# One load for the projection's matrix, and the last matrix in pieces of 9, 4 and 1 blocks, in a decoding transformer layer

## The chip, the core and the metric

The kernel runs on one core of a Trainium2 chip. The core has five engines, each with its own stream of instructions: TensorE (PE: matmuls into PSUM, with weight loads, PEld, that overlap them), VectorE (DVE), ScalarE (ACT), GpSimd (POOL) and SyncE (SP, which here only issues DMAs). They are tied together by semaphores. The metric is the device time in microseconds (us); lower is better.

## What is computed

One token passes through one layer of attention over a long cache, and then through a block of normalisation, mixing and MLP. `_layernorm` subtracts the mean and divides by the standard deviation; `_gelu` is the tanh form. All inputs are bfloat16.

```python
# x [1,1,512], k_cache and v_cache [1,8,16384,128], wq [512,4096], wo [4096,512]
q = (x @ wq).reshape(B, Sq, 32, 128).transpose(0, 2, 1, 3)      # x normalised
k, v = repeat(k_cache, 4, axis=1), repeat(v_cache, 4, axis=1)
p = softmax(einsum("bhqd,bhkd->bhqk", q, k) * 128 ** -0.5)
o = einsum("bhqk,bhkd->bhqd", p, v)
A = o.transpose(0, 2, 1, 3).reshape(B, Sq, 4096) @ wo
h = x + A
# B of the normalised h, with w1, w2 [512,512], w3 [512,1792], w4 [1792,512]
...
x1 = x + hs
h2 = _gelu(_layernorm(x1) @ w3) @ w4
out = h + (x1 + h2)
```

With one token the shifted parts of the mixing (`hs`) are all padding, so `hs` is zero, and neither w1 nor w2 is read. What has to be read is the cache (67 MB), wq and wo (4 MB each), and w3 and w4 (1.75 MB each).

## The kernel before

**Loads.** All large loads are issued by SP and go through one data queue, in order: wq, the keys and values of four pairs of heads in turn, then wo, w3 and w4. `load` (line 487) gives every load its name, its destination and its key; a load name has a semaphore of its own, which rises by 16 when the load has landed. wo goes where the keys' first half was (`kb[0]`), w3 and w4 where the second half was (`kb[1]`), so they are issued when VectorE has transposed the last pair's keys out of those buffers. The constants `WO`, `W3`, `W4` (lines 375 to 378) cut the matrices into loads, in units of rows for each partition: wo into 28 and 4 of 32 rows (of 512 columns), w3 into one load, w4 into pieces of 7, 5 and 2 of 14 blocks (of 512 columns, 1 KB for each partition). `piece` tells which load a row or block is in.

**The loops.** For each of four pairs TensorE multiplies transposed keys with the queries (line 666), VectorE and ScalarE make the softmax, TensorE multiplies with the values (line 703), and the result is gathered (lines 714 to 751). TensorE's stream of this part is one loop with registers (`_tensor`, line 176).

**The end.** Behind the loop TensorE first runs *unread* matmuls, whose result nobody reads (line 527): `P.spin(6)` (line 792) makes a loop of 6 passes with two of them in each. Then come:

- the projection: 32 matmuls of `o_b` with wo (line 795), in four column groups of the array, which add up into four 32-partition groups of one PSUM bank; a copy to `osum` (799), and 4 matmuls with `row32` (801) that fold the four groups into the row's layout, 128 partitions by 128 columns;
- the residual and the sums of the row (`row_sums`, 538), more unread matmuls (two of line 527, and a wide one in fp32 of 512 columns, line 535), the centred row `hc` (809);
- 16 matmuls with w3 (815), the variance (`variance`, 556), `xsum` = h + x1 (820), again a wide unread matmul (384 columns), two GELU activations (825), each followed by a transpose on VectorE (829) that makes one half of `hcol`, the columns for w4: blocks 0 to 6 from the first half, 7 to 13 from the second;
- one matmul that starts the output row in `n_ps` with `xsum` (833);
- w4's first 7 blocks: 7 matmuls of 512 columns into `O_ps[1]` in four column groups (838), a copy to `osum` (841), and 4 matmuls that fold it into `n_ps` (846);
- w4's other 7 blocks: for each of them four matmuls of 128 columns, straight into `n_ps` (852);
- two copies of halves of the result, on ACT (857) and DVE (859), the output write (860), and VectorE's wait for it (862).

An fp32 matmul shows as two in the profile (two passes).

**The branch near the end.** `pe(None, ...)` (line 844) and `dve(None)` (832) mark places at which the engine's stream has a compare-and-branch that is never taken back to the loop (`pe_pair`, line 360); its wait (`late`, an activation on ACT, line 842) comes in front of it.

**Semaphores of the engines.** `emit` (line 114) gives each engine one semaphore, that rises with each instruction that somebody waits for; an operation with `own=` counts on another one of that engine. [...]

Of the kernel before, what the change touches and what calls it, by code (L numbers as in the profile page):

```python
# [10 lines left out]
ACTF = mybir.ActivationFunctionType  # L11
# [13 lines left out]
class Program:  # L25
# [88 lines left out]
    def emit(self):  # L114
        for ops in self.ops.values():
            for o in ops:
                for d in o.deps:
                    d.needed = True
        told = {self.place(o) for e in ("PE", "DVE") for o in self.ops[e] if o.needed and o.at}
        for e in ("PE", "DVE"):  # L120
            for o in self.ops[e]:
                o.needed = o.needed or (o.at is not None and self.place(o) in told)
        for e, ops in self.ops.items():
            sems, n = {}, {}
            for o in ops:
                if o.dma is None and o.needed:
                    if o.own not in sems:
                        name = f"e_{e}" if o.own is None else f"e_{e}_{o.own}"
                        sems[o.own] = self.ctx.enter_context(self.nc.semaphore(name))
                    n[o.own] = n.get(o.own, 0) + o.worth  # L130
                    o.sem, o.val = sems[o.own], n[o.own]
        self.nc.switch_bb("body", parent=None)
        for e, eng in (("SP", self.nc.sync), ("ACT", self.nc.scalar), ("POOL", self.nc.gpsimd)):
            self._run(eng, self.ops[e], {})
        self._vector()
        self._tensor()
# [235 lines left out]
NCH = D // 128  # L372
FQ = FM // 4
NHC = FM // 128
WO = ((0, 28), (28, 32))
VP = 1
W3 = ((0, 4),)
W4 = ((0, 7), (7, 12), (12, 14))
NEAR = 7
BLOCK = (0, 2, 1, 3)  # L380
PAIRS = HKV // 2
RPARTS = 9
# [8 lines left out]
def bass_sequential_preLN__gqa_block_cached__mixer_s_mlp__decode_kernel(  # L391
# [13 lines left out]
    with ExitStack() as ctx:  # L405
        sb = lambda name, shape, dt: ctx.enter_context(nc.sbuf_tensor(name, shape, dt))
        ps = lambda name, shape, dt: ctx.enter_context(nc.psum_tensor(name, shape, dt))
        P = Program(nc, ctx)
# [19 lines left out]
        row32 = sb("row32", [128, 32], FP32)  # L428
# [21 lines left out]
        osum = sb("osum", [128, D], FP32)  # L450
# [13 lines left out]
        def late(words, dt=BF16):  # L464
            nonlocal taken
            lo, taken = taken, taken + words * (2 if dt is FP32 else 1)
            part = kt[:, lo:taken]
            return part.bitcast(FP32) if dt is FP32 else part

        o_f, hr, xsum = late(32, FP32), late(128, FP32), late(128, FP32)  # L470
        o_b, hg = late(32), late(FQ)
        hc = late(NCH * 32).rearrange("p (k u) -> p k u", u=32)
        hcol = late(NHC * 32).rearrange("p (m u) -> p m u", u=32)
        fin = late(256)[0:64, :]
        wq_sb, wo_sb = vb, kb[0]
        w3_sb = kb[1][:, 0:NCH * FM].rearrange("p (k f) -> p k f", k=NCH)
        w4_sb = kb[1][:, NCH * FM:2 * NCH * FM].rearrange("p (m c) -> p m c", m=NHC)
# [4 lines left out]
        O_ps = [banks[:, 2, :], banks[:, 3, :]]  # L482
        A_ps, mn_ps = banks[:, 4, :], banks[:, 5, :]
        m_ps, n_ps = mn_ps[:, 0:256], mn_ps[:, 256:512]


        def load(name, dst, src, key, by="SP", also=()):
            P.op(by, lambda e: e.dma_start(dst, src), w=[key, *also], dma=name)  # L488
# [18 lines left out]
        def dve(fn, r=(), w=(), bank=()):  # L507
            return P.op("DVE", fn, r, w, bank)

        def act(fn, r=(), w=(), bank=()):  # L510
            return P.op("ACT", fn, r, w, bank)
# [4 lines left out]
        def pe(fn, r=(), w=(), bank=(), also=()):  # L516

            return P.op("PE", fn, r, w, bank, also=also)

        def piece(cuts, m):  # L520
            return [lo <= m < hi for lo, hi in cuts].index(True)

        def copies(col, n):

            return col.to_broadcast([col.shape[0], n])

        P.unread = lambda e: e.matmul(banks[:, 7, :], copies(xn[:, 0:1], 128), copies(xn[:, 0:1], 512),  # L527
                                      start=True, stop=True)
# [45 lines left out]
        for n, (lo, hi) in enumerate(((0, 2048), (2048, NCH * HQ * DH))):  # L574
# [13 lines left out]
            r=["ident", "x4"], w=["quarter"])  # L588
        pe(lambda e: e.matmul(O_ps[0][:, 0:128], quarter[:, :, :].rearrange("p q u -> p (q u)"), x4[:, :],
                              start=True, stop=True), r=["quarter"], w=[("O", 0)], bank=[("O", 0)])  # L590
# [8 lines left out]
             r=["ident_f"], w=["swapped"])  # L599

        dve(lambda e: e.tensor_reduce(row32[:, :], ident_f[:, :].rearrange("p (c r) -> p r c", c=4), AX.X, ALU.add),
            r=["ident_f"], w=["row32"])
        dve(lambda e: e.tensor_reduce(maskdd[:, :], ident_f[:, :].rearrange("p (n d) -> p d n", d=4), AX.X, ALU.add),
            r=["ident_f"], w=["maskdd"])
# [6 lines left out]
        for z, m, key, mk in ((zo, rowgh, "zo", "rowgh"), (zd, maskgh, "zd", "maskgh")):  # L611
# [5 lines left out]
            r=["hT", (("st", 0), 0), (("st", 0), 6)] + [("v", 0), ("v", 1)], w=["xn"])  # L617
# [3 lines left out]
        for i, key in enumerate(keys):  # L621
            P.part("query", i)
            for k in range(NCH):
                pe(lambda e, k=k: e.matmul(row[:, bass.ds(P.b, 512)], copies(xn[:, k:k + 1], 128),  # L624
                                           wq_k[:, k, bass.ds(P.c, REP * DH)], start=(k == 0), stop=(k == NCH - 1)),
                   r=["xn"], also=[("v", 0), ("v", 1)], w=["n" if key == "mn" else key], bank=[key])
        P.part()
        for g in range(2):
            half = banks[64 * g:64 * g + 64, PAIRS * g:PAIRS * g + PAIRS, :].rearrange("p j c -> p (j c)")
            for b in range(2):  # L630
# [3 lines left out]
                    r=["n" if x == "mn" else x for x in keys[PAIRS * g:PAIRS * g + PAIRS]], w=["qcol"],  # L634
                    bank=keys[PAIRS * g:PAIRS * g + PAIRS])
# [35 lines left out]
        both = dict(bank=[("s", 0), ("s", 1)])  # L671
# [104 lines left out]
        act(lambda e: e.activation(scr[0:1, 1:2], mean4[0:1, 0:1], ACTF.Gelu_apprx_tanh), r=["mean4"], w=["scr"])  # L776
        for n, (lo, hi) in enumerate(WO):
            load(f"wo{n}", wo_sb[:, lo * D:hi * D], A_wo.rearrange("(p r) c -> p (r c)", p=128)[:, lo * D:hi * D],
# [4 lines left out]
        w4_in = B_w4.rearrange("(p m) c -> p m c", p=128)  # L783
        for n, (lo, hi) in enumerate(W4):
            load(f"w4{n}", w4_sb[:, lo:hi, :], w4_in[:, lo:hi, :], ("r", 1, len(W3) + n))
# [3 lines left out]
            r=[("o_m", j) for j in range(PAIRS)], w=["o_f"])  # L789
        dve(lambda e: e.tensor_copy(o_b[:, :], o_f[:, :]), r=["o_f"], w=["o_b"])  # L790

        P.spin(6)
        for r_ in range(32):
            q = r_ % 4
            pe(lambda e, r_=r_, q=q: e.matmul(O_ps[0][32 * q:32 * q + 32, :], copies(o_b[:, r_:r_ + 1], 32),  # L795
                                              wo_sb[:, r_ * D:(r_ + 1) * D], start=(r_ < 4), stop=(r_ >= 28)),
               r=["o_b", ("r", 0, piece(WO, r_))], w=[("O", 0)], bank=[("O", 0)])
        h_ps, hkey = banks[:, 6, :], "spare0"
        dve(lambda e: e.tensor_copy(osum[:, :], O_ps[0][:, :]), r=[("O", 0)], w=["osum"] + [("osum", c) for c in range(4)], bank=[("O", 0)])
        for q in range(4):  # L800
            pe(lambda e, q=q: e.matmul(h_ps[32 * q:32 * q + 32, 0:128], copies(row32[:, 0:1], 32),
                                       osum[:, q * 128:(q + 1) * 128], start=True, stop=True),
               r=["osum", "row32"], w=[hkey], bank=[hkey])
# [6 lines left out]
            r=["hT", (S, 0)], w=["hc"])  # L810


        for k in range(NCH):
            for q in range(4):
                pe(lambda e, k=k, q=q: e.matmul(s_ps[32 * q:32 * q + 32, 0, 0:FQ], hc[:, k, :],  # L815
                                                w3_sb[:, k, q * FQ:(q + 1) * FQ], start=(k == 0), stop=(k == NCH - 1)),
                   r=["hc", ("r", 1, piece(W3, k))], w=[("s", 0)], bank=[("s", 0)])
# [3 lines left out]
            r=["hr", "xs", (S, 6)], w=["xsum"])  # L821
        unread_f(384)
        for n in range(2):
# [9 lines left out]
        pe(lambda e: e.matmul(  # L833
            n_ps[:, 0:128], swapped[:, :], xsum[:, :], start=True, stop=False, skip_group_check=True),
           r=["swapped", "xsum"], w=["n"], bank=["mn"])
        for m in range(NEAR):
            q = m % 4
            pe(lambda e, m=m, q=q: e.matmul(O_ps[1][32 * q:32 * q + 32, :], hcol[:, m, :], w4_sb[:, m, :],
                                            start=(m < 4), stop=(m >= NEAR - 4)),
               r=[("hcol", 2 * m // NHC), ("r", 1, len(W3) + piece(W4, m))], w=[("O", 1)], bank=[("O", 1)])  # L840
        dve(lambda e: e.tensor_copy(osum[:, :], O_ps[1][:, :]), r=[("O", 1)], w=["osum"], bank=[("O", 1)])
        act(lambda e: e.activation(hg[:, 0:256], hcol[:, 0:8, :].rearrange("p m u -> p (m u)"), ACTF.Identity),
            r=[("hcol", 1)], w=["late", ("hg", 0), ("hg", 1)])
        pe(None, r=["late"])
        for o in range(4):
            pe(lambda e, o=o: e.matmul(
                n_ps[32 * o:32 * o + 32, 0:128], copies(row32[:, 0:1], 32),
                osum[:, BLOCK[o] * 128:(BLOCK[o] + 1) * 128], start=False, stop=False,
                skip_group_check=True), r=["osum", "row32"], w=["n"], bank=["mn"])
        for m in range(NEAR, NHC):  # L850
            for o in range(4):
                pe(lambda e, m=m, o=o: e.matmul(
                    n_ps[32 * o:32 * o + 32, 0:128], hcol[:, m, :], w4_sb[:, m, BLOCK[o] * 128:(BLOCK[o] + 1) * 128],
                    start=False, stop=(m == NHC - 1),
                    skip_group_check=True),
                   r=["late", ("r", 1, len(W3) + piece(W4, m))], w=["n"], bank=["mn"])
        act(lambda e: e.activation(fin[:, 0:128], n_ps[0:64, 0:128], ACTF.Identity),
            r=["n"], w=[("fin", 0)], bank=["mn"])
        dve(lambda e: e.tensor_copy(fin[:, 128:256], n_ps[64:128, 0:128]), r=["n"], w=[("fin", 1)])
        P.op("SP", lambda e: e.dma_start(out[0, 0:1, :].rearrange("o (q j) -> (o q) j", q=2), fin[31:33, :]),  # L860
             r=[("fin", 1), ("fin", 0)], w=["out"], dma="out")
        P.op("DVE", lambda e: e.nop(), r=["out"])
# [31 lines left out]
```

## Time and profile before

| | |
|---|---|
| median of three runs | 189.71 us (189.6 to 189.81) |
| the profiled execution: device time | 189.68 us |
| the profiled execution: span of the instructions | 188.2 us |
| TensorE busy | 127.9 us (68%) |
| VectorE busy | 107.9 us (57%) |
| ScalarE, GpSimd busy | 14.2 us (8%), 9.4 us (5%) |
| read from HBM | 79.17 MB, 421 GB/s over the span |

The profile is of one execution. Its times count from the start of the span. In the rows, `out<-in` names the tiles written and read; many late tiles live in the buffer `kt`, and w3 and w4 in `kb`, so they appear under those names. The rows of a timeline have the start, the duration, the engine, the line and the operation, and in brackets how long the engine was idle before and what ended it. SPq is SP's queue of instructions, PEldq TensorE's. The page's list of DMA issues has the size in KB and the median time from issue to landing.

### The profile page before, as it was taken

Reading aid. Unit: us, or ns where it says so; the run is one execution under the profiler, and the core shown is the slowest. Engines: PE = TensorE matmul, PEld = TensorE weight load, DVE = VectorE, ACT = ScalarE, POOL = GpSimd, SP = SyncE. Lnnn points to the kernel's source line nnn. Section 1 sums busy time; section 2 is a strip of 40 time slices with the busy share of each in tenths; the row PEclk is TensorE's granted clock in tenths of the full one; section 3 lists DMA queues with packets and bytes.
Section 4 is the critical chain, followed back from the end, with each engine's and each line's share of the span. In section 5 each row is a group of like instructions: output and inputs, shape, how many; then the busy total and the mean of one; then the engine's idle time right before and its main releaser. Section 6 shows DMA issues by size and latency. Waiting matters only on the chain.

```text
span 188.2 us, 2422 instructions
## 1 busy us (share of the span) xinstructions
PE 127.9 (68%) x776; PEld 53.2 (28%) x780; DVE 107.9 (57%) x138; ACT 14.2 (8%) x32; POOL 9.4 (5%) x21
## 2 busy tenths in 40 slices
PE   1019800699965703999775019997986999797984
PEld 1003300243422201344332003442432334343332
DVE  4300651999645009998450069994659894453254
ACT  3000000000020200000012000000220000320012
POOL 1700000000000020000002100000003000000010
PEclk9999995599997885599999855999998899999999
DMA  6999999999999999888999999997999998799994
GB/s 240 457 418 446 446 446 446 446 446 446 446 446 446 446 446 446 362 376 376 446 446 446 446 446 446 446 446 334 446 446 446 557 446 348 334 471 421 404 410 179
DMA packets 2461, 79.19 MB, mean 421 GB/s; under 512 B 282, under 2 KB 284, under 8 KB 924
## 3 DMA queue, kind: packets, MB, share of 16 engines
q1 hardware_dynamic: 2452, 79.17, 97.9%
q8 instruction: 1, 0.02, 0.0%
q10 hardware_dynamic: 8, 0.00, 0.0%
HBM read 79.17 MB, written 0.00 MB: 421 GB/s over the span
## 4 chain that ended last, share of the span: by engine, by line
DMA 44%; PE 31%; DVE 14%; issue 8%; POOL 1%; SPq 0%; ACT 0%; POOLq 0%; DVEq 0%; ACTq 0%
DMA kb<-in_A_k_cache_dram 30%; PE banks L666 18%; DMA vb<-in_A_v_cache_dram 15%; DVE kt L647 8%; PE banks L527 4%; PE banks L703 4%; DVE pt L692 1%; DVE mx L676 1%; PE banks L795 1%; PE banks L660 1%; DVE od L733 1%; PE banks L680 1%; PE banks L535 1%; PE banks L815 1%; SPq L488 0%
## 5 line engine op out<-in xcount | busy, mean ns | idle before, releaser
L647 DVE STREAM_TRANSPOSE kt<-kb 128x1024 int32<-128x1024 int32 (+1 forms) x49 | 71.8, 1534 | 31.9 <-DMA kb<-in_A_k_cache_dram 31.9
L666 PE MATMUL banks<-kt,qn 128*128 x256 | 67.9, 417 | 0.0
L666 PEld LDWEIGHTS banks<-kt,qn 128*128 x256 | 26.4, 103 | 40.0 <-issue 21.1
L527 PE MATMUL banks<-xn 128*128 128x512 bf16 x90 | 22.0, 381 | 0.6 <-issue 0.6
L660 PE MATMUL banks<-qn 128*128 128x512 bf16 x8 | 3.7, 464 | 26.5 <-DVE kt L647 26.2
L703 PE MATMUL banks<-vb,pt 128*32 128x512 bf16 x256 | 16.3, 411 | 0.0
L624 PE MATMUL banks<-vb,xn 128*128 x32 | 9.2, 459 | 9.6 <-DVE xn L615 9.6
L688 ACT ACTIVATE p_sb<-banks,bias 128x1024 bf16<-128x1024 f32 x4 | 4.5, 1114 | 126.0 <-DVE nmh L684 126.0
L692 DVE STREAM_TRANSPOSE pt<-p_sb 64x1024 bf16<-64x1024 bf16 x8 | 9.9, 1239 | 5.4 <-ACT p_sb L688 5.3
L527 PEld LDWEIGHTS banks<-xn 128*128 128x128 bf16 x94 | 8.8, 99 | 12.1 <-issue 4.5
L676 DVE TENSOR_REDUCE mx<-banks 128x1 f32<-128x1024 f32 x4 | 4.9, 1225 | 9.0 <-PE banks L666 9.0
L703 PEld LDWEIGHTS banks<-vb,pt 128*32 128x32 bf16 x256 | 8.0, 103 | 6.3 <-issue 2.0
L631 DVE STREAM_TRANSPOSE kt<-banks 64x1024 f32<-64x1024 f32 x4 | 4.8, 1227 | 7.2 <-PE banks L624 7.2
L660 PEld LDWEIGHTS banks<-qn 128*128 128x128 bf16 x8 | 0.8, 100 | 28.3 <-issue 28.0
L722 POOL TENSOR_TENSOR osum<-osum 128x256 f32<-128x256 f32 x3 | 2.2, 723 | 127.5 <-ACT osum L719 127.5
L624 PEld LDWEIGHTS banks<-vb,xn 128*128 128x128 bf16 x32 | 3.7, 115 | 14.7 <-issue 12.3
L738 PE MATMUL banks<-od,zo 128*32 128x128 f32 x8 | 1.6, 285 | 7.3 <-POOL od L724 6.1
L680 PE MATMUL banks<-mxd,mean 128*128 128x128 f32 x8 | 2.0, 326 | 5.3 <-DVE mxd L677 5.3
L719 ACT ACTIVATE osum<-banks,rowc 128x128 f32<-128x128 f32 x12 | 3.4, 368 | 20.7 <-PE banks L703 20.7
L615 DVE TENSOR_SCALAR xn<-hT,st 128x4 bf16<-128x4 f32 x1 | 0.3, 290 | 6.5 <-DMA vb<-in_A_wq_dram 6.5
L711 PE MATMUL banks<-acc,zd 128*32 128x1 f32 x8 | 0.9, 180 | 4.1 <-DVE pt L692 4.0
L568 POOL TENSOR_TENSOR st<-st,expo 128x1 f32<-128x1 f32 (+1 forms) x2 | 1.3, 636 | 41.3 <-DVE st L566 41.3
(88 smaller groups left out, 46.3 us busy)
## 6 DMA issues: line engine op xcount, KB each, us to landing
kb<-in_A_k_cache_dram SPq DMA_DIRECT2D x2, 4096.0 KB, 20.4
vb<-in_A_wq_dram SPq DMA_DIRECT2D x1, 3584.0 KB, 11.7
kb<-in_A_wo_dram SPq DMA_DIRECT2D x1, 3584.0 KB, 28.5
kb<-in_B_w_dram SPq DMA_DIRECT2D x1, 1792.0 KB, 24.2
kb<-in_B_w_dram SPq DMA_DIRECT2D x1, 896.0 KB, 26.0
kb<-in_B_w_dram SPq DMA_DIRECT2D x1, 640.0 KB, 27.1
vb<-in_A_wq_dram SPq DMA_DIRECT2D x1, 512.0 KB, 3.6
kb<-in_A_wo_dram SPq DMA_DIRECT2D x1, 512.0 KB, 29.4
```

The lines of the kernel that those rows point to most:

```text
L527: P.unread = lambda e: e.matmul(banks[:, 7, :], copies(xn[:, 0:1], 128), copies(xn[:, 0:1], 512), start=True, stop=True)
L624: pe(lambda e, k=k: e.matmul(row[:, bass.ds(P.b, 512)], copies(xn[:, k:k + 1], 128), wq_k[:, k, bass.ds(P.c, REP * DH)], start=(k == 0), s ...
L631: dve(lambda e, g=g, b=b, half=half: e.transpose(qcol[64 * g:64 * g + 64, 2 * b:2 * b + 2, :, :].rearrange("p e m u -> p (e m u)"), half.r ...
L647: P.op("DVE", lambda e, t=t, n=n, at=at: e.transpose(kt[:, t * KP:(t + n) * KP].bitcast(I32), kb_all[:, at:at + n * KP].bitcast(I32)), r=[ ...
L660: pe(lambda e: e.matmul(row[:, bass.ds(P.y, 512)], copies(none, 128), copies(none, 512), start=True, stop=False, skip_group_check=True), r ...
L666: pe(lambda e, n=n: e.matmul(row[:, bass.ds(P.y, 512)], qn[:, n, bass.ds(P.q, 128)], key_piece(P.k, n), start=False, stop=(n == 3), skip_g ...
L676: dve(lambda e: e.tensor_reduce(mx[:, :], s_all, AX.X, ALU.max), r=[("s", 0), ("s", 1)], w=["mx"], **both)
L680: pe(lambda e: e.matmul(m_ps[:, 0:128], mean4[:, :], mxd[:, :], start=True, stop=True), r=["mxd", "mean4"], w=["m"], bank=["mn"])
L688: act(lambda e: e.activation(p_sb[:, :], s_all, ACTF.Exp, bias=bias[:, 0:1], scale=float(SCALE), accum_out=acc[:, :]), r=[("s", 0), ("s", ...
L692: dve(lambda e, g=g: e.transpose(pt[64 * g:64 * g + 64, :, :, g, :], p_sb[64 * g:64 * g + 64, :]), r=["p"], w=["pt"])
L703: pe(lambda e, l=l, ct=ct, ch=ch: e.matmul(O_ps[0][32 * ct:32 * ct + 32, :], pt[:, l, ch, :, :].rearrange("p g u -> p (g u)"), tiles[:, l ...
L719: act(lambda e, c=c: e.activation(osum[:, c * 128:(c + 1) * 128], O[:, c * 128:(c + 1) * 128], ACTF.Identity, scale=rowc[:, c:c + 1]), r=[ ...
```

## The change

Four things are changed. wo comes in one load. w4 comes in pieces of 9, 4 and 1 blocks. All 14 blocks of w4 are multiplied straight into the row in `n_ps`, four matmuls of 128 columns each, so that the path over `O_ps[1]` and `osum` is gone, with the activation `late`; the branch stands between blocks 8 and 9. The two copies of the result count on one semaphore that both engines share, `both`, so that the output write has one wait. The loop of unread matmuls ahead of the projection has 8 passes.

```diff
@@ emit
+        both, told_both = {}, {}
         for e, ops in self.ops.items():
-            sems, n = {}, {}
+            own_sems, own_n = {}, {}
             for o in ops:
+                sems, n = (both, told_both) if o.own == "both" else (own_sems, own_n)
                 if o.dma is None and o.needed:
...
-WO = ((0, 28), (28, 32))
+WO = ((0, 32),)
 VP = 1
 W3 = ((0, 4),)
-W4 = ((0, 7), (7, 12), (12, 14))
-NEAR = 7
+W4 = ((0, 9), (9, 13), (13, 14))
...
-        P.spin(6)
+        P.spin(8)
...
-        for m in range(NEAR):
-            q = m % 4
-            pe(lambda e, m=m, q=q: e.matmul(O_ps[1][32 * q:32 * q + 32, :], hcol[:, m, :], w4_sb[:, m, :],
-                                            start=(m < 4), stop=(m >= NEAR - 4)),
-               r=[("hcol", 2 * m // NHC), ("r", 1, len(W3) + piece(W4, m))], w=[("O", 1)], bank=[("O", 1)])
-        dve(lambda e: e.tensor_copy(osum[:, :], O_ps[1][:, :]), r=[("O", 1)], w=["osum"], bank=[("O", 1)])
-        act(lambda e: e.activation(hg[:, 0:256], hcol[:, 0:8, :].rearrange("p m u -> p (m u)"), ACTF.Identity),
-            r=[("hcol", 1)], w=["late", ("hg", 0), ("hg", 1)])
-        pe(None, r=["late"])
-        for o in range(4):
-            pe(lambda e, o=o: e.matmul(
-                n_ps[32 * o:32 * o + 32, 0:128], copies(row32[:, 0:1], 32),
-                osum[:, BLOCK[o] * 128:(BLOCK[o] + 1) * 128], start=False, stop=False,
-                skip_group_check=True), r=["osum", "row32"], w=["n"], bank=["mn"])
-        for m in range(NEAR, NHC):
+        for m in range(NHC):
+            if m == W4[0][1]:
+                pe(None, r=[("hcol", 1)])
             for o in range(4):
                 pe(lambda e, m=m, o=o: e.matmul(
                     n_ps[32 * o:32 * o + 32, 0:128], hcol[:, m, :], w4_sb[:, m, BLOCK[o] * 128:(BLOCK[o] + 1) * 128],
                     start=False, stop=(m == NHC - 1),
                     skip_group_check=True),
-                   r=["late", ("r", 1, len(W3) + piece(W4, m))], w=["n"], bank=["mn"])
-        act(lambda e: e.activation(fin[:, 0:128], n_ps[0:64, 0:128], ACTF.Identity),
-            r=["n"], w=[("fin", 0)], bank=["mn"])
-        dve(lambda e: e.tensor_copy(fin[:, 128:256], n_ps[64:128, 0:128]), r=["n"], w=[("fin", 1)])
+                   r=[("hcol", 2 * m // NHC), ("r", 1, len(W3) + piece(W4, m))], w=["n"], bank=["mn"])
+        P.op("ACT", lambda e: e.activation(fin[:, 0:128], n_ps[0:64, 0:128], ACTF.Identity),
+             r=["n"], w=[("fin", 0)], own="both")
+        P.op("DVE", lambda e: e.tensor_copy(fin[:, 128:256], n_ps[64:128, 0:128]), r=["n"], w=[("fin", 1)], own="both")
```

## The prediction

> **What bounds the kernel now.** I read the page first, then the last five microseconds of the timeline, then the issues and landings of the weight loads.
>
> ```profile
> span 188.2 us, 2422 instructions
> q1 hardware_dynamic: 2452, 79.17, 97.9%
> DMA 44%; PE 31%; DVE 14%; issue 8%; POOL 1%; SPq 0%; ACT 0%; POOLq 0%; DVEq 0%; ACTq 0%
> ```
>
> The one data queue is busy for 97.9% of the span. All 79 MB must pass through it, so unless a part of the change opens a hole in it or shortens its sum, the time can move only by what happens after the last byte. The end of the timeline (start, duration, engine, and in brackets what ended the idle time):
>
> ```profile
> 183.49 1.04 DVE L829 STREAM_TRANSPOSE kt<-kt 128x224 bf16<-128x224 bf16 x2 [0.44 <-ACT kt L825]
> 184.16 0.61 PE L838 MATMUL banks<-kb,kt 128*32 128x512 bf16 x7 [0.18 <-DVE kt L829]
> 184.82 0.69 DVE L841 COPY osum<-banks 128x512 f32<-128x512 f32 x1 [0.29 <-PE banks L838]
> 185.56 0.43 PE L846 MATMUL banks<-osum,row 128*32 128x128 f32 x8 [0.79 <-DVE osum L841]
> 185.81 0.78 PE L852 MATMUL banks<-kb,kt 128*32 128x128 bf16 x28
> 186.29 0.12 PEld L852 LDWEIGHTS banks<-kb,kt 128*32 128x32 bf16 x8 [0.19 <-DMA kb<-in_B_w_dram]
> 186.64 0.27 ACT L857 ACTIVATE kt<-banks 64x128 bf16<-64x128 f32 x1 [1.66 <-PE banks L852]
> 186.64 0.29 DVE L859 CAST kt<-banks 64x128 bf16<-64x128 f32 x1 [1.13 <-PE banks L852]
> 186.98 0.33 SPq L860 DMA_DIRECT2D out_dram<-kt  x1
> ```
>
> The sixth row decides: at 186.29 TensorE had finished 20 of its 28 last matmuls and stood still for 0.19 us until the last piece of w4 landed. The chain of compute (transposes, seven wide matmuls, copy, fold, 20 matmuls) is done 0.19 us before the data. From 186.29 on the path is fixed: the last matmuls, two copies side by side, the output write, the end at 188.15. So two terms set the end: when the last piece lands, and what stands behind it.
>
> **The landings.** Issue times on SP's queue, and the microseconds from issue to landing (last column of the page's list of DMA issues):
>
> ```profile
> 147.74 0.33 SPq L488 DMA_DIRECT2D kb<-in_A_wo_dram  x1
> ...
> 148.12 0.43 SPq L488 DMA_DIRECT2D kb<-in_A_wo_dram  x1
> ...
> 157.64 0.33 SPq L488 DMA_DIRECT2D kb<-in_B_w_dram  x1
> ...
> 158.02 0.43 SPq L488 DMA_DIRECT2D kb<-in_B_w_dram  x1
> ...
> 158.49 0.44 SPq L488 DMA_DIRECT2D kb<-in_B_w_dram  x1
> ...
> 158.98 0.44 SPq L488 DMA_DIRECT2D kb<-in_B_w_dram  x1
> ```
> ```profile
> kb<-in_A_wo_dram SPq DMA_DIRECT2D x1, 3584.0 KB, 28.5
> kb<-in_B_w_dram SPq DMA_DIRECT2D x1, 1792.0 KB, 24.2
> kb<-in_B_w_dram SPq DMA_DIRECT2D x1, 896.0 KB, 26.0
> kb<-in_B_w_dram SPq DMA_DIRECT2D x1, 640.0 KB, 27.1
> ...
> kb<-in_A_wo_dram SPq DMA_DIRECT2D x1, 512.0 KB, 29.4
> kb<-in_B_w_dram SPq DMA_DIRECT2D x1, 256.0 KB, 27.3
> ```
>
> Sums give the landings: wo 176.24 and 177.52, w3 181.84, w4 184.02, 185.59 and 186.28. Each was issued more than 24 us earlier, so they wait in line, and the distance between two landings is the price of a load in the queue: 4 KB for each partition (512 KB) 1.28, 14 KB 4.32, 7 KB 2.18, 5 KB 1.57, 2 KB 0.69. Between 14 and 2 KB the slope is (4.32 - 0.69)/12 = 0.30 us per KB, which leaves 0.69 - 0.60 = 0.09 us for each load whatever its size. The other three fit within the rounding (1.29, 2.19, 1.59).
>
> **Part 1, wo in one load.** One load of 32 KB replaces 28 and 4 KB: one fixed 0.09 less. The bytes are the same. wo then lands whole at 177.52 - 0.09 = 177.43, and w3 at 181.75. SP's second issue (0.43 us) goes too; it costs nothing now, because its load waited 29.4 us. *Last landing: -0.09* (between 0, if the fixed part is rounding, and -0.14).
>
> What it costs is on TensorE: all 32 projection matmuls now wait for 177.43, where the first 28 started on 176.24.
>
> ```profile
> 174.79 1.91 PE L527 MATMUL banks<-xn 128*128 128x512 bf16 x8
> ...
> L159 PEldq EVENT_SEMAPHORE x1: 96/96/96, 176.2 to 176.2; - x1
> ...
> 176.63 1.91 PE L795 MATMUL banks<-kb,kt 128*32 128x512 bf16 x32
> ...
> 180.76 1.11 PE L535 MATMUL banks<-mean 128*128 128x512 f32 x2
> 181.14 0.40 ACT L809 ACTIVATE kt<-hT,st 128x128 bf16<-128x128 f32 x1 [15.24 <-DVE st L554]
> 181.98 0.94 PE L815 MATMUL banks<-kb,kt 128*32 128x448 bf16 x16
> 182.97 0.85 ACT L825 ACTIVATE kt<-banks,st 128x224 bf16<-128x224 f32 x2 [1.43 <-PE banks L815]
> ```
>
> The unread matmuls ahead of it go at (1.91 - 0.38)/7 = 0.22 us each, 0.38 being the length of one. Two more passes of two are +0.87, so the projection starts at 176.63 + 0.87 = 177.50 by the loop and near 177.5 by the landing: both agree, and I take +0.9. The whole chain behind it (osum, the row sums, hc) moves by 0.9. At L815 some comes back: now it starts at 181.98, 0.44 after hc was ready (181.54), behind the wide unread matmul and w3's landing at 181.84; w3 is early afterwards. The second half of that unread matmul can end no later than its modelled end, 181.87, so L815 moves by 0.7 to 0.9, and the transposes, which end at 184.08 and 184.53 (two in 1.04 from 183.49), end at 184.8 to 185.0 and 185.2 to 185.45.
>
> **Part 2, w4 in 9, 4 and 1 blocks straight into the row.** By the same price the pieces take 0.09 + 0.30 x 9 = 2.79, 1.29 and 0.39, together 4.47, as 7, 5 and 2 KB do (2.19 + 1.59 + 0.69). They land at 181.75 + 2.79 = 184.54, 185.83 and 186.22. The 1 KB piece is not in the trace. Its price is bounded by the 2 KB row: at best half of it, 0.345, at worst all of it, 0.69. That puts the last landing between -0.14 and +0.21 against 186.28. I take 0.39, on the line through five sizes, so -0.09 stays the sum for the landing.
>
> [...]
>
> On TensorE the wide matmuls, the osum copy (0.69) and the fold (0.43) go. For each block there are four matmuls of 128 columns:
>
> ```profile
> L852 PE MATMUL banks<-kb,kt x28: 219/219/231, 185.8 to 186.4; 128*32 128x128 bf16 x28
> ...
> 185.99 0.28 PE banks L852 x20
> 186.29 0.33 PE banks L852 x8
> ```
>
> The first 20 start at 185.81 and are over at 186.27 (185.99 + 0.28). With 0.22 for the last one, five groups of four stand 0.24/4 = 0.06 us apart. Blocks 0 to 6 start at 184.9 to 185.05 (piece one landed at 184.54) and take 0.42; blocks 7 and 8 need the second transpose (185.45 at the latest) and are through by 185.45 + 0.05 + 0.12 = 185.6. That is 0.2 before piece two at 185.83. Blocks 9 to 12 take 0.24 from there, to 186.1, and wait again for 186.22. So the 0.9 of part 1 is hidden by the landings of pieces two and three. Without that cover it would cost all of it.
>
> Behind the last landing stand four matmuls and not eight: one group, *-0.06*. The late activation (0.42 on ScalarE) and the copy are off the path already.
>
> **Part 3, one semaphore.** SP waits for ACT in an instruction of its own and for DVE in the DMA's.
>
> ```profile
> L159 SPq EVENT_SEMAPHORE x1: 17/17/17, 186.9 to 186.9; - x1
> ```
>
> That wait is 17 ns long and sits while DVE is ending (186.64 + 0.29 = 186.93; the write starts at 186.98). At most 0.05 can be won, at least 0; I take *-0.01*, as DVE ends last either way.
>
> **Sum.** -0.09 - 0.06 - 0.01 = -0.16. The profiled execution took 189.68 with a span of 188.15, the median of the runs is 189.71, 0.03 above it. 189.71 - 0.16 = **189.55**, that is -0.08%. What a measurement here can tell from nothing is about 0.2%, 0.38 us.
>
> **The rivals.**
>
> *Code that is not there (slower).* The page has one instruction load, and this is when it ran:
>
> ```profile
> L360 PEldq COMPARE_BRANCH  x1: 78/78/78, 185.0 to 185.0; - x1
> ...
> DMA  0900000000000000000000000000000000000000
> ...
> q8 instruction: 1, 0.02, 5.1%
> ```
>
> The second and third are of the window 186 to 187.5: the 16 KB start in its second slice, at about 186.05, and take 0.051 x 16 x 1.5 = 1.22 us, until 187.28, which is 2.27 after TensorE's branch at 185.02. If the branch sets it off, and if TensorE's code after the change reaches into that block, the last matmuls must wait for it. The code does grow: 7 + 8 + 28 = 43 matmuls with their weight loads become 56, 26 instructions more. The branch would come behind the second transpose, near 185.4; the code lands at 187.67, and the last four matmuls start there and not at 186.29: +1.38 - 0.06, **191.0**. It decides as soon as one of the last 26 instructions lies behind the block's end. Against it: now the last matmuls run at 186.29, a microsecond before that block is there, so they don't need it, and whether 26 more do isn't in any row. 8%. [...]
>
> *The chain of compute binds.* If the branch now between blocks 8 and 9 stalls (before, 0.47 us of waiting for osum, 185.09 to 185.56, lay behind it and could hide a stall), or the chain moves by more than 0.9. Slack: ready at 185.6 and 0.24 of work before 186.22, so 0.4. A stall of 0.8 to 1.0, about double what could hide before, would end at +0.4 to +0.6 less 0.07: **190.15**. The profile shows no such stall. 7%.
>
> *The 1 KB piece costs what 2 KB do.* +0.21 - 0.07: **189.85**, no change by the measure. 11%. A piece dearer than one of twice its size (about 1 us, +0.6 - 0.07: 190.25) gets 1%, with that row against it.
>
> *More is won*: half the 2 KB price (-0.14), 0.07 for the group, all 0.05 at the semaphore, and a little at the output: **189.4**; past the bound only if the runs scatter low too. 10%.
>
> **The numbers.** 63% for the forecast. Past 0.2% on the slow side lie the first two rivals, 15% (the dear piece is within the rounding); on the fast side 7%, from the last rival and scatter (the three runs span 0.21); 78% no change. The range 189.3 to 190.1 leaves out the first rival and a part of the second.
>
> **What would show it.** One wo load landing near 177.4; L795 starting near 177.5; the transposes ending by 185.45; TensorE released by a DMA twice, near 185.85 and 186.2, with four matmuls behind the last; the output write at about 186.83; a span near 188.0. I am wrong if the last weight load is released by a transpose or by nothing visible, if the instruction load stands just ahead of the last matmuls, or if the last piece lands over 0.6 us behind its predecessor.

## The result, and the profile after

The change made the kernel slower: 192.64 us (median of 5 runs, 192.34 to 193.06) against 189.73 (5 runs, 189.6 to 189.97), a ratio of 1.0146, 95% interval 1.0124 to 1.0169. (The ratio goes with its interval and is not the quotient of the two medians, which is 1.0153.) I had forecast 189.55, with a range up to 190.1. The page of the changed kernel, whose profiled execution took 193.06, the longest of the five, has these lines:

```profile
span 191.6 us, 2456 instructions
q1 hardware_dynamic: 2308, 79.17, 96.3%
DMA 68%; DVE 28%; issue 2%; SPq 1%; PE 0%; DVEq 0%
```

The bytes are the same and the queue is as busy in time (96.3% of 191.6 is 184.5 us, 97.9% of 188.2 is 184.2). The loss is at the end. The timeline of the changed kernel, same columns as before:

```profile
184.82 1.06 DVE L830 STREAM_TRANSPOSE kt<-kt 128x224 bf16<-128x224 bf16 x2 [0.28 <-ACT kt L826]
185.46 0.77 PE L841 MATMUL banks<-kb,kt 128*32 128x128 bf16 x36
186.47 0.22 PEld L841 LDWEIGHTS banks<-kb,kt 128*32 128x32 bf16 x13 [0.41 <-DMA kb<-in_B_w_dram]
186.47 0.35 PE L841 MATMUL banks<-kb,kt 128*32 128x128 bf16 x12 [0.24 <-DMA kb<-in_B_w_dram]
189.68 0.41 PE L841 MATMUL banks<-kb,kt 128*32 128x128 bf16 x8 [2.86 <-issue]
189.69 0.14 PEld L841 LDWEIGHTS banks<-kb,kt 128*32 128x32 bf16 x7 [3.00 <-issue]
190.14 0.27 ACT L846 ACTIVATE kt<-banks 64x128 bf16<-64x128 f32 x1 [4.98 <-PE banks L841]
190.14 0.29 DVE L848 CAST kt<-banks 64x128 bf16<-64x128 f32 x1 [4.26 <-PE banks L841]
190.46 0.33 SPq L849 DMA_DIRECT2D out_dram<-kt  x1
```

Up to the fourth row all goes in the order that I had written. Then TensorE does 12 matmuls, loads the weights of the 13th, and stands still for 2.86 us. The bracket says "issue": nothing in the profile that an engine can wait for (a semaphore, a landing) ended it. The place is odd too. It lies inside block 12, before the wait for the last piece, which stands at block 13.

The branch of TensorE, and the instruction load as a share of 16 DMA engines in the window 187 to 188.5:

```profile
L362 PEldq COMPARE_BRANCH  x1: 78/78/78, 186.0 to 186.0; - x1
...
q8 instruction: 1, 0.02, 5.5%
```

The load is in this window, so it starts no earlier than 187, a microsecond behind the branch (185.95), and it takes 0.055 x 16 x 1.5 = 1.3 us. In the trace it is one packet of 16,384 bytes, from 187.03 to 188.36. The first instruction after the stall is at 189.68, 3.7 us behind the branch.

The landings, from the issue times on SP's queue and the times to landing:

```profile
148.32 0.33 SPq L489 DMA_DIRECT2D kb<-in_A_wo_dram  x1
...
158.20 0.33 SPq L489 DMA_DIRECT2D kb<-in_B_w_dram  x1
...
158.58 0.43 SPq L489 DMA_DIRECT2D kb<-in_B_w_dram  x1
...
159.06 0.42 SPq L489 DMA_DIRECT2D kb<-in_B_w_dram  x1
...
159.52 0.43 SPq L489 DMA_DIRECT2D kb<-in_B_w_dram  x1
```
```profile
kb<-in_A_wo_dram SPq DMA_DIRECT2D x1, 4096.0 KB, 29.7
...
kb<-in_B_w_dram SPq DMA_DIRECT2D x1, 1792.0 KB, 24.1
kb<-in_B_w_dram SPq DMA_DIRECT2D x1, 1152.0 KB, 26.6
...
kb<-in_B_w_dram SPq DMA_DIRECT2D x1, 512.0 KB, 27.4
kb<-in_B_w_dram SPq DMA_DIRECT2D x1, 128.0 KB, 27.2
```

They are at 178.02, 182.3, 185.18, 186.46 and 186.72. The times to landing are rounded to 0.1; the landings themselves in the trace are 178.05, 182.35, 185.13, 186.42 and 186.72, so the last three loads stand 2.78, 1.29 and 0.30 apart, where the line through the rows of before had 2.79, 1.29 and 0.39. So the landings are as forecast, the small piece a little cheaper; this execution was 0.6 late as early as wo (177.43 forecast), in the keys and values ahead of it.

### The profile page after: what moved, and what is told of

It is laid out like the page before. It is cut to its first block, busy times and chain, and to the rows that moved or that the text cites. A ratio compares the mean times of both kernels' runs of the same rounds, so it can differ in the third digit from the quotient of the medians.

```text
span 191.6 us, 2456 instructions
## 1 busy us (share of the span) xinstructions
PE 128.5 (67%) x793; PEld 53.3 (28%) x797; DVE 109.0 (57%) x137; ACT 13.8 (7%) x31; POOL 9.3 (5%) x21
## 3 DMA queue, kind: packets, MB, share of 16 engines
q1 hardware_dynamic: 2308, 79.17, 96.3%
## 4 chain that ended last, share of the span: by engine, by line
DMA 68%; DVE 28%; issue 2%; SPq 1%; PE 0%; DVEq 0%
DMA kb<-in_A_k_cache_dram 53%; DVE kt L648 28%; DMA kb<-in_B_w_dram 14%; SPq L489 1%; PE banks L841 0%; DVE kt L848 0%; DVEq L161 0%; SPq L161 0%
## 5 line engine op out<-in xcount | busy, mean ns | idle before, releaser
L528 PE MATMUL banks<-xn 128*128 128x512 bf16 x94 | 22.8, 381 | 0.6 <-issue 0.6
L841 PE MATMUL banks<-kb,kt 128*32 128x128 bf16 x56 | 1.5, 233 | 3.3 <-issue 2.9
L800 DVE COPY osum<-banks 128x512 f32<-128x512 f32 x1 | 0.7, 692 | 4.7 <-PE banks L796 4.7
## 6 DMA issues: line engine op xcount, KB each, us to landing
kb<-in_A_wo_dram SPq DMA_DIRECT2D x1, 4096.0 KB, 29.7
kb<-in_B_w_dram SPq DMA_DIRECT2D x1, 1792.0 KB, 24.1
kb<-in_B_w_dram SPq DMA_DIRECT2D x1, 128.0 KB, 27.2
```

## The experiments

**The theory.** This is how I read the stall: behind some entry TensorE's code is not there until the 16 KB have been loaded that follow the branch, and in after it could be used 3.73 us behind it (185.95 and 189.68). I call both blocks: the code that is there already, which ends at that entry, and the 16 KB behind it. No view shows blocks as such; the entry is counted. Counted in the compiled program, labels with it, TensorE's list has 457 entries before and 483 after. (The count is mine and stands in no profile. The traces show how many instructions are left behind the stall, and the edits show how many come or go.) In the last rows above 8 matmuls and 7 weight loads were still to come, so by this reading the block ends behind entry 483 - 15 = 468. The kernel before has 11 to spare. The rivals: the stall belongs to the direct matmuls, or to the new place of the branch, whatever the length. One thing no run separates: in the kernel this branch carries a `branch_hint` (line 360 in before), which no run leaves out, so whether the hint or the branch as such holds the load back stays open.

All times against the kernel before on the same chip; "outside" is the device time less the span, over the timed runs. In the kernel before it is 1.4 to 1.6.

| run | entries | median us | ratio, 95% interval | outside, us |
|---|---|---|---|---|
| e1, before and 10 more | 467 | 190.42 | 1.0034 [1.0020, 1.0047] | 1.9 to 2.1 |
| e2, before and 12 more | 469 | 192.11 | 1.0125 [1.0107, 1.0143] | 1.4 to 1.5 |
| e3, after, branch first | 483 | 191.19 | 1.0069 [1.0050, 1.0087] | 1.4 to 2.1 |
| e4, after, 16 fewer | 467 | 193.97 | 1.0229 [1.0198, 1.0260] | 2.6 to 4.0 |
| e5, e4 mended | 467 | 191.62 | 1.0088 [1.0063, 1.0114] | 2.5 to 3.6 |
| e6, e5, branch at block 0 | 466 | 189.80 | 1.0010 [0.9994, 1.0026] | 1.4 to 2.3 |
| e7, wo alone | 457 | 190.18 | 1.0024 [1.0014, 1.0034] | 1.4 to 1.6 |
| e8, semaphore alone | 457 | 189.66 | 0.9997 [0.9987, 1.0007] | 1.4 to 1.6 |
| e9, cuts and semaphore | 457 | 189.53 | 0.9988 [0.9976, 1.0001] | 1.4 to 1.5 |
| e10, after mended | 466 | 189.62 | 0.9993 [0.9980, 1.0005] | 1.4 to 1.5 |
| e11, e10, wo in two | 466 | 189.63 | 0.9992 [0.9981, 1.0004] | 1.4 to 1.5 |
| e12, after, branch at block 0 | 482 | 191.75 | 1.0104 [1.0083, 1.0124] | 1.4 to 1.5 |

**e1 and e2: only the length.** In the kernel before, small matmuls that nobody reads, in the time in which TensorE waits for the osum copy:

```diff
+        for _ in range(5):        # e2: range(6)
+            pe(lambda e: e.matmul(banks[:, 7, 0:32], copies(xn[:, 0:1], 128), copies(xn[:, 0:1], 32),
+                                  start=True, stop=True), r=["xn"], w=["spare1"])
         dve(lambda e: e.tensor_copy(osum[:, :], O_ps[1][:, :]), r=[("O", 1)], w=["osum"], bank=[("O", 1)])
```

> The kernel before with 5 small unread matmuls more (10 instructions with their weight loads), put where TensorE waits for the osum copy, 0.7 us of idle time. Theory (code): in the trace of after TensorE stands still behind the 13th weight load and the 12th matmul past its branch, at 186.82, and the instruction block is loaded from 187.03 to 188.36. Counted over the whole of TensorE's program that place is behind 26 - 15 = 11 instructions more than the kernel before has. 10 more still fit: 189.7 us, no change. Rival (the form): the stall belongs to the direct matmuls or to the branch's new place, so nothing happens here either, 189.7.

> The same with 6 small unread matmuls (12 instructions). Theory (code): one instruction, the last matmul, lies past the block's end; it waits until 3.7 us after the branch (after: branch at 185.95, matmuls go on at 189.68), so until about 188.7 in place of 186.36: +2.4, 192.1 us. Rival (the form): as with 10, 189.7 to 189.8.

e2's timeline, and its branch:

```profile
185.71 0.78 PE L855 MATMUL banks<-kb,kt 128*32 128x128 bf16 x27
186.19 0.12 PEld L855 LDWEIGHTS banks<-kb,kt 128*32 128x32 bf16 x8 [0.20 <-DMA kb<-in_B_w_dram]
188.71 0.27 PE L855 MATMUL banks<-kb,kt 128*32 128x128 bf16 x1 [2.22 <-issue]
...
L360 PEldq COMPARE_BRANCH  x1: 78/78/78, 184.9 to 184.9; - x1
```

27 of the 28 last matmuls run in time, the weights of the 28th are loaded, and that one matmul waits until 188.71, 3.8 us behind the branch. This kernel has nothing of the change in it, and only two instructions more than e1. The rival of the form falls. 192.11 is what the theory gave. From branch to first held-up instruction it is 3.7 us in after, 3.8 here and 3.4 in e12 below.

e1's expectation missed: no matmul waits (its span is 188.3), but it is 0.65 us slower. The time lies outside the span. The closing instructions of the program, which the profile doesn't show, come behind entry 467 as well; so I take it that they too wait for the block when the spare room is used up.

**e3 and e12: the branch's place, at full length.** In after:

```diff
+        pe(None)                                     # e3; e12 below
         P.spin(8)
...
-            if m == W4[0][1]:
-                pe(None, r=[("hcol", 1)])
+        pe(None, r=[("r", 1, len(W3))])              # e12, ahead of the loop over m
```

> After, with TensorE's branch ahead of the unread matmuls of the projection (near 174.2) and not between blocks 8 and 9. Theory (code): the block is asked for at 174.2 and there by 178, long before it is needed: no stall, so about -0.16 against before, plus 0 to 0.6 for 16 KB that one DMA engine now has to carry between the weights (16 KB at the 26 GB/s of an engine): 189.55 to 190.15 us. Rival (the form): the stall stays, 192.6; rival (the branch itself stalls): it would stand at 174 and be hidden, 189.55.

> After as it is, 14 instructions past the block's end, with only the branch moved ahead of block 0 (behind the landing of w4's first piece, 184.7 to 185.1). Theory (the block comes 3.75 us after the branch): the matmuls go on near 188.6 and not at 189.68, 1.1 sooner: 191.5 us. Rival (the block is asked for when TensorE runs into its end): the stall ends where it did in after, 192.6.

e12's timeline and branch:

```profile
185.91 0.40 PE L840 MATMUL banks<-kb,kt 128*32 128x128 bf16 x13 [0.27 <-DMA kb<-in_B_w_dram]
188.01 0.12 PEld L840 LDWEIGHTS banks<-kb,kt 128*32 128x32 bf16 x7 [1.88 <-issue]
188.01 0.29 PE L840 MATMUL banks<-kb,kt 128*32 128x128 bf16 x7 [1.70 <-issue]
...
L362 PEldq COMPARE_BRANCH  x1: 78/78/78, 184.6 to 184.6; - x1
```

The stall ends at 188.01, 3.4 us behind the branch. The branch is about 1.4 earlier than in after (184.6 and 186.0) and the end of the stall 1.67 (188.01 and 189.68), while TensorE stops at the block's end only 0.5 earlier (at about 186.3 here, 186.8 in after). So the end of the stall goes with the branch, and not with TensorE's running into the block's end. Seven pairs remain of 482 entries: 468 again, the place that after and e2 gave.

In e3 the matmuls wait for landings alone, and yet it is slower than my price of 0.6 for the 16 KB: this expectation missed too. Its last matmuls, two of its landings, the page's count of instruction loads, and the share of the one in the window 177.9 to 179.2:

```profile
186.72 0.69 PE L840 MATMUL banks<-kb,kt 128*32 128x128 bf16 x36 [0.79 <-DMA kb<-in_B_w_dram]
187.88 0.56 PE L840 MATMUL banks<-kb,kt 128*32 128x128 bf16 x20 [0.48 <-DMA kb<-in_B_w_dram]
...
kb<-in_B_w_dram SPq DMA_DIRECT2D x1, 1792.0 KB, 25.5
...
kb<-in_B_w_dram SPq DMA_DIRECT2D x1, 128.0 KB, 28.6
...
q8 instruction: 2, 0.03, 0.1%
...
q8 instruction: 1, 0.02, 5.1%
```

w3 takes 25.5 and not 24.1, the last piece 28.6 and not 27.2: the four loads behind wo take 1.3 to 1.4 longer than in after, wo itself 0.1 (29.8 and 29.7). The block starts to move in the window 177.9 to 179.2, about when wo lands (the projection starts at 178.33) and well ahead of w3 (its matmuls start at 183.93), and takes 0.051 x 16 x 1.3 = 1.06 us; which engines it holds up isn't shown. And the block itself starts only 3.5 us or more behind the branch (174.4). VectorE's branch, which stands within 1.2 us of TensorE's in the kernels before (183.87 and 185.02) and after (185.20 and 185.95), comes there 0.38 behind the start of the first transpose; that starts at 185.44 here, so the branch is near 185.8, an estimate, and not the one that this load follows. What the second load of this run follows the runs don't show. So with the early branch of e3 no code stalled and the data came up to 1.4 us late; with the late one of after TensorE stood still for 2.86 us.

**e4, e5, e6: after, made to fit.** Unread matmuls are left out until the list has 467 entries:

```diff
-            unread(1)            # softmax
-            unread(2)            # gather
-        P.spin(8)
+        P.spin(16, 1)            # e4; e5 and e6: P.spin(8, 1)
-        unread(2)                # ahead of row_sums
-        unread_f(512)
+        unread(1)
-        unread_f(384)
+        unread(1)
...
-            if m == W4[0][1]:    # e6 only
-                pe(None, r=[("hcol", 1)])
+        pe(None, r=[("hcol", 0)])
```

> After with 16 instructions of TensorE fewer: the unread matmuls of the gather, of the softmax and of the row sums are left out, the two wide fp32 ones become one bf16 one each, and the loop ahead of the projection has 16 passes of one in place of 8 of two. The whole program then ends one instruction ahead of the block's end. Theory (code): no stall, 189.55 us, or up to 0.3 more if TensorE's clock suffers from the idle time. Rival (the form, or the branch's new place): 192.6.

> e4 again without the fault of its loop (one matmul a pass took 0.41 us a pass, so 16 passes were 2.4 us too long): 8 passes of one. The program fits in the block by one instruction, the branch stays between blocks 8 and 9. Theory (two prices of the block): no stall at the matmuls, but the block comes 3.75 us after the branch and the program's closing instructions, which begin 0.3 after the span's end, need it: branch near 185.7 gives 189.45 against 188.3, so about 1.1 more than 189.55: 190.5 to 190.9 us. Rival (only the matmuls can be held up by code): 189.55 to 189.7.

> e5 with the branch ahead of block 0, behind the first transpose. Theory: branch near 184.75, the block is asked for behind the last weight packets (they end near 185.65, the load begins 1.05 after the branch), and there by 188.5: the closing waits 0 to 0.2, so 189.5 to 189.8 us; this is the change without its two faults. Rival (the stall belongs to the direct matmuls): as e5 or slower.

e4 was ill made and missed its forecast: a pass of its loop takes 0.41 us with one matmul as with two, and the projection starts 2.4 late. In e5 that is gone:

```profile
178.22 2.38 PE L794 MATMUL banks<-kb,kt 128*32 128x512 bf16 x32 [0.22 <-DMA kb<-in_A_wo_dram]
...
185.90 1.21 PE L838 MATMUL banks<-kb,kt 128*32 128x128 bf16 x56 [0.19 <-DVE kt L827]
...
L362 PEldq COMPARE_BRANCH  x1: 78/78/78, 186.4 to 186.4; - x1
```

All 56 direct matmuls run through in 1.21 us: with a list that fits, there is no stall in them here. Its profiled execution has a span of 188.7, hardly over before, and a time of 192.34: 3.6 us lie outside. By the theory the branch at 186.4 is too late for the closing. The median is 0.7 over the upper end of the forecast, whose branch was to stand at 185.7; that the closing begins 0.3 behind the span's end was an assumption there, which no profile holds. e6 moves the branch ahead of block 0, whose first matmul is at 185.85, and 1.8 us of the median go. The projection takes 2.38 here in place of the 1.91 of before, with unread matmuls left out ahead of it; e6 has such a lapse at another place (last section). The lapses, and a closing that still waits in some runs (up to 2.3 outside), are what I put down for e6 being level with before; no run separates them.

**e7, e8, e9: parts alone, in before.**

```diff
-WO = ((0, 28), (28, 32))
+WO = ((0, 32),)                                      # e7, with P.spin(8)
-W4 = ((0, 7), (7, 12), (12, 14))
+W4 = ((0, 7), (7, 13), (13, 14))                     # e9
+             r=["n"], w=[("fin", 0)], own="both")    # e8 and e9: both copies, with the code in emit
```

> The kernel before with wo in one load and 8 passes, nothing else. The chain of compute moves by 0.7 to 0.9, and with the wide matmuls, copy and fold still in it it is behind the last landing by 0.4 to 0.6. Theory (the block counts in the closing too): the branch moves to about 185.75, the block comes at 189.5, the closing waits for it: 190.3 to 190.9 us. Rival (only the chain counts): 190.1 to 190.3. My prediction's reading that merging the load gains 0.09 on the last landing is seen in the landings' distances.

> The kernel before with the two copies of the result on one shared semaphore, nothing else. My prediction: -0.01 (0 to -0.05): 189.7 us, no change that can be told; a write that starts more than 0.1 later behind the copies would show a cost of the shared semaphore.

> The kernel before with w4 cut in 7, 6 and 1 blocks and the shared semaphore; wide matmuls, fold, branch and wo as they were, TensorE's program as long as before. Prediction's terms: one group of four matmuls fewer behind the last landing (-0.06), the 1 block piece at 0.30 as the trace of after has it (pieces together 0.04 less), the semaphore -0.02: -0.12, 189.6 us. If the small piece were dear here, 189.8 or more.

e7's chain at the end:

```profile
184.89 0.61 PE L838 MATMUL banks<-kb,kt 128*32 128x512 bf16 x7
185.54 0.69 DVE L841 COPY osum<-banks 128x512 f32<-128x512 f32 x1 [0.25 <-PE banks L838]
186.29 0.42 PE L846 MATMUL banks<-osum,row 128*32 128x128 f32 x8 [0.79 <-DVE osum L841]
186.53 0.57 PE L852 MATMUL banks<-kb,kt 128*32 128x128 bf16 x28
```

The chain is 0.72 later (185.54 for 184.82), the 28 matmuls run without a wait for a landing, and the time is up by 0.42: the rival that only the chain counts was right. The branch waits for `late`, which starts 0.77 later than before (185.33 for 184.56); with 11 entries to spare that harms nothing here. So one wo load costs 0.4 in the old form. e8: nothing that can be told, as forecast. e9 is 0.2 under before, with an interval that just takes in no change; it has the lowest median of all runs, without one direct matmul.

**e10 and e11: the change without its two faults.** The branch as in e12, and 16 instructions fewer with most unread matmuls kept:

```diff
-        dve(... tensor_copy(osum[:, :], O_ps[0][:, :]) ...)
+        dve(... tensor_copy(osb[:, :], O_ps[0][:, :]) ...)      # osb and row32b in bf16: the fold in one pass
-            unread(1)            # softmax
-        unread_f(512)
+        unread(1)
-        unread_f(384)
...
+WO = ((0, 28), (28, 32))         # e11 only, with P.spin(6)
```

> After with both faults of the code taken away and the unread matmuls mostly kept: 16 instructions fewer (the first fold in bf16 takes one pass in place of two, one wide unread matmul becomes a bf16 one, the other and the softmax's one are left out), and the branch ahead of block 0, behind the landing of w4's first piece (near 184.65). Theory: the block is asked for behind the last weight packets and there by 188.4; landings -0.11 against before, one group -0.06, semaphore -0.02: -0.19, 189.55 us, plus 0 to 0.4 in runs in which the closing still waits. Rival (the direct matmuls or one wo load cost something themselves): over 189.9 with no wait for code in the trace.

> e10 with wo in two loads and 6 passes as before. The projection starts 0.9 earlier, but all behind it waits for w4's pieces, so only the 0.07 of the merged load are lost: 189.6 us. If it is clearly faster than e10, the one load still costs time through the later chain.

e10's end:

```profile
184.63 0.69 PE L841 MATMUL banks<-kb,kt 128*32 128x128 bf16 x36 [0.34 <-DMA kb<-in_B_w_dram]
185.80 0.54 PE L841 MATMUL banks<-kb,kt 128*32 128x128 bf16 x20 [0.49 <-DMA kb<-in_B_w_dram]
186.40 0.27 ACT L846 ACTIVATE kt<-banks 64x128 bf16<-64x128 f32 x1 [2.23 <-PE banks L841]
186.72 0.33 SPq L849 DMA_DIRECT2D out_dram<-kt  x1
...
L362 PEldq COMPARE_BRANCH  x1: 78/78/78, 184.5 to 184.5; - x1
```

This is what I had forecast for after: TensorE waits for landings alone, and the write goes out at 186.72 (186.98 in before). This execution is the shortest of its twelve (189.31); the median is 189.62 against 189.73. The intervals of e10 and e11 take in no change, and so does the -0.16 that I had summed; they are 3 us under after. Whether wo comes in one load or two makes no difference in this form.

## Why the prediction was wrong

**The step that failed** is the rival "code that is not there", to which I gave 8%, and the price of 0 for the branch in the forecast. I had the condition (code that reaches past what is there waits for the load behind the branch), the 26 instructions and the rows (one instruction load, at 186.06, a microsecond behind the branch at 185.02), and then wrote that "whether 26 more do isn't in any row". The rows of before don't hold where the block ends, so 8% was a guess at an unknown. e2 shows that 12 more are enough. The argument against it, that the last matmuls of before ran ahead of the load, told only that they fitted, not by how much: 11.

**The price of that rival was too small.** I let TensorE go on when the 16 KB had moved, 2.27 behind the branch. It went on 3.4 (e12), 3.7 (after) and 3.8 (e2) behind it. In after that is 189.68, 3.39 behind the 186.29 of before, and 0.41 us of matmuls follow (0.33 in before). That makes the +3.4 of the profiled execution. 0.6 of it is the lateness which that execution had from wo on; without it 2.8 to 2.9 are left, as between the medians.

**The branch's place is a second fault**, that I saw only as a stall of the branch itself. With the code made to fit, the kernel with the branch between blocks 8 and 9 (e5) is still 1.9 us over before, and most of it lies outside the span; moving the branch alone to block 0 (e6) takes 1.8 of it away. That the closing instructions wait for the same block is my estimate from times, as the profile doesn't hold them. In after TensorE goes on 1.32 us after the block has moved (188.36 and 189.68). In e5 the block starts to move at about 188.2 and takes 0.051 x 16 x 1.7 = 1.39 us; 1.3 behind that is 190.9, 2.2 behind the end of the span, and the time outside of this execution (3.64) is 2.2 more than the 1.45 that is usual. In the profiled executions of e1, e4 and e6 0.7, 1.1 and 0.8 are added outside. In e7, ten entries shorter than e1, nothing is (1.38): by the theory the closing still fits there.

**What held.** The price of a load in the queue: by the landings of the trace a piece of 9 KB takes 2.78 (2.79), 4 KB 1.29 (1.29), 1 KB 0.30 (0.39). The last lies under my lower bound of 0.345, half of the 0.69 for 2 KB; that 0.69 came of rounded rows, and the landings of before (185.61 and 186.25 in the trace) give 0.63. The sum for the landing had a small slip: the pieces by the line end at 186.22, which is 0.06 ahead of 186.28 and not 0.09. Counted from wo's issue the last landing came 0.11 earlier (38.40 in after, 38.51 in before). No run shows the price of about 1 us for the small piece that the rival of 1% counts with (+0.6): in the full queue 128 KB took 0.30. One wo load moves the chain by 0.7 (0.7 to 0.9), which costs 0.42 in the old form (e7) and nothing in the direct one (e10 against e11). The semaphore: nothing (e8). The sum of -0.16 is what e10 has to within its interval (-0.13, from -0.38 to +0.1), and it is no more than the scatter.

## What to carry to other kernels

This kernel's last microseconds also depended on where its code ended: 10 instructions more cost 0.65 us (e1), 12 more 2.3 (e2), many times what the change was to win, and in e2 a single matmul lay past the end. So before instructions are added to an engine with a long program, count its list, look in the profile for instruction loads and for the branch ahead of them, and see with a few instructions more, as in e1 and e2, where the spare room ends. Here the place of the branch went with the time at which the code came: with the branch ahead of the projection, in the full queue, the later data were up to 1.4 us late (e3), and with the branch behind block 8 TensorE stood still for 2.86 us (after) or 2.2 us more lay outside the span (e5). What worked was both at once, code short enough to fit and a branch some 3.4 us ahead of the span's end (184.5 and 187.9 in e10).

## What the runs showed of the hardware that I had not expected

- The block of 16 KB moves in 1.06 us (e3), 1.22 (before), 1.33 (after) and 1.39 (e5). It begins 1.05 us behind the branch in before, 1.08 in after and 1.8 in e5, where the weights are through (their last packets end at 185.74 in before and 186.28 in after, and the block begins at 186.06 and 187.03), but 3.5 or more behind it in e3, where the queue was full, and there the later loads take 1.3 to 1.4 us longer. That is more than twice what 16 KB cost at an engine's mean rate in before, an estimate (0.62 us at 26 GB/s, 421 over 16 engines). In after TensorE goes on 1.32 us after the block has moved. The branch is never taken here, and yet TensorE stands still behind the same entry, 468, in after, e2 and e12.
- TensorE's granted clock was 0.51 over w3's matmuls in e6, where unread matmuls are left out. The windows of these 16 matmuls in e6 and in e10, which leaves out others (length, busy time and count of each engine, granted clock, share of DMA, GB/s):

```profile
182.80:184.60 1.80, 1.77 (x17) 0.62 (x18) 0.76 (x4) 0.03 (x1) 0.70 (x1) 0.51 0.98 405
```
```profile
182.20:183.20 1.00, 0.94 (x16) 0.34 (x16) 0.41 (x3) 0.00 (x0) 0.69 (x1) 1.00 0.99 415
```

The clock is 0.51 in the first and 1.00 in the second, and the matmuls take 1.69 us and 0.94. Which fillers are left out doesn't settle it alone. e5 leaves out the same ones as e6, and there the lapse is in the projection, at a clock of 0.79; e5's projection window, its w3 matmuls, and e6's projection:

```profile
178.20:180.60 2.40, 2.38 (x32) 0.98 (x32) 0.00 (x0) 0.00 (x0) 0.00 (x0) 0.79 0.94 400
...
183.65 0.94 PE L813 MATMUL banks<-kb,kt 128*32 128x448 bf16 x16 [0.45 <-ACT kt L807]
...
177.88 1.91 PE L794 MATMUL banks<-kb,kt 128*32 128x512 bf16 x32 [0.69 <-DMA kb<-in_A_wo_dram]
```

With all the fillers, in before and in after, the projection and w3's matmuls take 1.91 and 0.94, at a clock of 1.00. So where these fillers were taken out to make room for code, the matmuls took 0.75 us more in e6 (w3) and 0.47 more in e5 (the projection); the two traces have the lapse at different places.
